# A planned order of steps replaced: LayerNorm, windowed attention and a gated layer on one core

## The chip, the core and the metric

The kernel runs on one core of a Trainium2 chip. The core has a matrix engine (TensorE, PE in the profile, with its weight loads as PEld), VectorE (DVE), ScalarE (ACT), GpSimd (POOL), and SyncE (SP), which here only issues DMAs. Each engine works through its own queue of instructions in order; an instruction that waits for another engine or for a DMA holds up all that stand behind it on its engine. The metric is the device time of one execution in microseconds.

## The reference

```python
h  = x + attention(layernorm(x)) @ wo       # x: 2048 x 512, 32 heads of 16
     # a query sees itself and the 255 keys before it
n  = layernorm(h)
h2 = h + (sigmoid(n @ w_gate) * (n @ w_up)) @ w_down     # 512 -> 1376 -> 512
```

All arrays are float32.

## The kernel before

**Numbers.** A float32 operand is held as two float16 halves: the cast (hi) and what the cast lost (lo). `mm3` (L356) does three matmuls for one product: hi·hi, hi·lo and lo·hi. So every operand needs a cast (L309 on ACT, L311 or, with a scale, L313 on DVE) and a subtraction (`subtract`, L316, on DVE or GpSimd; or, with a scale, a scalar_tensor_tensor on DVE: L752, L853, L966, L983).

**Attention.** The 2048 rows are cut into 8 blocks of 256 queries, and the heads into 8 groups. A block is normalized (`layernorm`, L489 to L504, then `split`), transposed, multiplied with wqkv (`do_qk`, `do_v`), and its rows are laid out anew through DRAM (`do_keys`, `do_queries`). For each half of the groups the scores are computed once with queries as rows (`do_s`, L652, tile sp), only to find each row's maximum (DVE, L639). `do_m` writes the maxima as two float16 halves (L659, L660), transposes them with a DMA (L664, tile mt) and puts them with a second DMA (L668) into spare rows of the queries' tile SQ. Then the scores are computed a second time with keys as rows (`do_st`: L703, L704, L705 and L714, tile stp), now with the maximum subtracted by the matmul itself. ACT takes exp (L681, tiles pa and pb), GpSimd zeroes what lies outside the window (`far`, L687, and `dia`, L692), and PE multiplies with the values (`do_pv`, L740, tile pvp, which has one buffer). Each of the 32 products of this kind is copied out as two halves rh ("raw": a cast, L309 or L313, then L752), which frees pvp for the next one. `do_o` transposes them back with a DMA (tile RT) and adds the halves (L770, tile OS). `do_wo` divides by the sum of the exps (L782, L784), splits the result (tile whl), transposes it with a DMA (tile oT, L533), multiplies with wo (L356, tile mmp) and adds the residual (L806).

**The second layer.** Its weights are split during the last attention block, once their largest value is known (`do_amax`, `scale`): w_gate through `do_T` (loads L952, cast, lo half L966 into tile Wg; four differences L976 on DVE or GpSimd, and their halves, L983, into Tg), w_up and w_down through `do_split` (tiles W0u and WD, L853). The first row tiles are normalized again (`do_ln2`) and multiplied with the first columns of both weights while attention still runs (`do_early`, tile sp from Wg and W0u). The other early products (`do_gu`) follow behind the last exp. From row tile 8 on, two tiles at a time go through `do_pair` and `do_group` (L1084), which does a 2 x 2 block product with 7 products instead of 8. `do_down` (L1244) multiplies with w_down, adds the residual (L1248) and stores.

**What sets the order.** Each of these pieces is a Python generator that yields once before each of its steps; with the yield it names the engines on which the step may run, what it needs, and what buffers it takes. The string `TABLE` (L64 to L224) lists all 4345 steps in order. `Order.run` reads it from left to right: a token is the name of a piece, a letter for the engine where there is a choice (a for ACT, v for DVE, g for GpSimd) and *n for n steps in a row.

```python
piece, (costs, needs, *rest) = self.live[name]
self.on = {"v": DVE_, "a": ACT_, "g": POOL_}[choice] if choice else next(iter(costs))
self.live[name][1] = piece.send(((0.0, self.on), *places))
```

No scheduler moves anything afterwards: the order of the table is the order on every engine. The costs that a piece yields, such as `4 * (n * 0.0031 + 0.15)` at L973 for the four subtractions L976 on GpSimd, were read by the planner that wrote the table. Here only the keys of `costs` are read.

Of the kernel before, what the change touches and what calls it, by code (L numbers as in the profile page):

```python
# [56 lines left out]
PE_, DVE_, ACT_, POOL_, DMA_ = ENGINES = "PE", "DVE", "ACT", "POOL", "DMA"  # L57
# [7 lines left out]
load_x0 load_x1 load_w0 load_w1 load_w3 load_w2 load_w4 load_w8 load_w9 load_x3 load_x2 load_w5 load_w10 load_w11 ln0 fill1 zeros0 ln0 ln1 load_w13 load_w7  # L65
load_w6 load_w15 load_x4 load_w14 load_x8 load_w12 load_x5 load_x6 ln0/a prep0/a ln0/a prep0/v*2 prep0/a prep0 ln1 ln0/v ln1/a prep0 warm1 ln0 ln1/a prep1/a
prep0 prep0/a ln0/v fill0*2 zeros1 ln1/g warm4 ln1 ln4 prep0 prep0/a prep0 prep0/a prep2/a prep0 ln1/a prep0/a prep0 ln4 ln4/v ln2 ln3 ln2 ln5 ln2/v prep2/a
warm3 qk0*2 qk1*2 qk0*3 qk1*2 qk0*3 ln3 prep1/a prep2/a*2 qk0/a prep2 ln3/v qk0 ln3/v ln2/a ln5 ln2/g ln3/g qk1*2 warm2 qk1*2 warm5 prep2 ln2 warm0 qk1/a qk1
prep1/a*2 ln2/v prep1 ln6 prep3/v prep2 warm7 ln3 prep1 warm6 queries2 queries0*2 queries3*3 queries1 queries2 load_x7 queries1*2 queries2 queries0 prep3/a*2
ln3/a qk4*5 qk5 qk4*3 qk5*6 ln4/a prep3/a prep2/a*2 prep2/g prep2/v ln7 prep3 prep2/v prep1 ln8 prep2/g fill2 prep2/a qk4/a prep2/a prep2/g fill2*4 ln4/g  # L70
prep2/v qk4 qk5 prep3*2 qk5/a prep2/a prep1/a qk5 v2*3 v0 prep2/v v2 v0 prep1 prep3/a prep1/a prep1 prep1/a prep1 v2/a prep1/a prep1 v0 qk3 warm8 qk3*2 v0 qk3
ln5/v v0/v qk3*3 qk2*2 qk3 qk2 queries5*2 amax0 queries7 amax2 queries7 amax1 queries7 queries4 queries6 queries4 queries6 queries4 queries6 qk2*5 qk3/a qk2/a
qk3 qk7*6 fill1 ln6 fill0*2 qk2 qk6 qk7*2 amax0/a qk7/v qk7 prep3/a prep3/g prep3/v keys0*2 amax3 queries5 keys0 qk6*6 v1 qk6 qk6/a v1*2 qk6 prep3/v amax2/v
ln9 prep3/v amax3/v prep3/v*2 v3 v1 v1/a amax1/a v3*2 ln4 v3 ln5/a ln4/a v3/a ln9 ln5/g ln8 fill1 ln7 ln6/a s0*3 s0.0 s0 s0.1 s0.2 s0*2 s0.3 s0.4 s0.5 s0*2 v4
s1 s0.6 s0.7 s1.0 amax4 keys1*2 keys0 amax6 s1*2 ln5 s1.1 s1.2 s2 s2.0 ln10 v4 s1 s1.3 s1*2 v4*2 s1.5 s1.4 open_work0 s1 s1.6 s1 s2 amax4/a ln6/a ln5/a ln10
ln6/g prep3/g v4/a ln7/a prep3/a s1.7 s2 s2.1 s2.2 qk8 s2 qk8 s2 s2.3 s2 qk8 s2.4 s2 s3 qk8 s2.5 qk8 s3 s2.6 qk8 s3.0 qk8 s3 s2 qk8 prep3/a qk8/a amax6/a ln11
s3.1 s3.2 s2.7 s3 qk9 s3*2 qk9 s3.3 s3.4 s3.5 s4 s4.0 s3 s3.6 qk8 qk9 s3 qk9*4 s4 qk9 s3.7 s4 qk10 s4 qk10 m0 s4.1 s4.2 s4.3 qk10 s4 s4.4 s4 qk10 s4 qk10*2 s4
qk10*2 amax7 qk9/a qk9 keys1 amax5 amax8 qk10/a amax5/a amax7/a m0*2 qk11 s4.5 s5 qk11 s4.6 s4.7 s5 qk11 s5.0 s5*2 qk11 qk10 qk11 s5.1 s5.2 qk11 s5 s6 qk11
s5.3 s5.4 s6.0 s5 qk11 s5.5 s6 s5 s6.1 s5.6 s5 s5.7 st0*2 ln6 qk11/a st0.0 st0.1 qk11 s6*2 st0 s6 st0 s6.2 ln7/a st0.2 st0.3 s6.3 s6.4 s6 s6.5 keys2*2 amax9
keys1 amax8/v amax11 st0*2 s7 s6*2 s7.0 s6.6 s6.7 ln6/a st0.5 ln7/g fill1 st0.4 v5 s7 st0.6 s7 st1 s7.1 s7.2 s7 ln7 st1 s7 st1.0 s7.3 s7 ln8/v s7.4 s7.5 st1  # L80
# [205 lines left out]
def tile_block(ctx, tc, x, wqkv, wo, wg, wu, wd, out):  # L286
# [1115 lines left out]
    n = 0  # L1402
# [54 lines left out]
```

## Time and profile before

| | |
|---|---|
| time, median of 3 runs | 781.17 us (779.52 to 781.47) |
| the profiled execution: its own time | 779.84 us |
| its span in the trace | 777.8 us |
| mean granted clock of PE | 0.993 |
| instructions | 18094 |
| busy: PE, DVE, ACT, POOL | 742.5, 600.7, 424.4, 346.8 us |

The span is the time between the first and the last instruction of the profiled execution; 2.0 us of its time lie outside. An engine's busy time is the time in which it worked at an instruction, waiting left out. A stretch of the span is given as a pair of times from its start. The granted clock is the share of full speed at which PE was allowed to run: 1.00 is full speed. In a row of the groups stand the line, the engine, the operation, what is written and read with its shape, the count, then the busy time and the mean in ns of one, and at last the idle time before them and what ended it. In a row of the waits stand the waiting engine, tile and line, behind the arrow what it waited for, then total, times and longest. In a row of the timeline stand start, duration, engine, line and, in brackets, the idle time just before.

### The profile page before, as it was taken

How to read it: one execution, taken by the hardware profiler on the slowest of the kernel's cores; microseconds unless marked ns; L12 is line 12 of the kernel's file. 1: busy time of each engine (PE TensorE's matmuls, PEld its weight loads, DVE VectorE, ACT ScalarE, POOL GpSimd, SP SyncE). 2: the span in 40 equal slices, each digit the busy share in tenths (PEclk: the TensorE clock that was granted, in tenths of full speed). 3: DMA queues.
4: the chain of work that ended last, by engine and by line, in shares of the span. 5: the costliest groups of instructions: out<-in, count | busy, mean ns of one | idle time of the engine just before them, and what ended most of it. 6: DMA issues, size and time to landing. Idle time of an engine off the chain costs nothing.

```text
span 777.8 us, 18094 instructions
## 1 busy us (share of the span) xinstructions
PE 742.5 (95%) x6714; PEld 468.1 (60%) x6714; DVE 600.7 (77%) x1772; ACT 424.4 (55%) x744; POOL 346.8 (45%) x437
## 2 busy tenths in 40 slices
PE   4899999999999999999997889999999999999998
PEld 4667767777787687786764444454544454545453
DVE  6969999989797887888889989993675757476552
ACT  6836889777787687887776725542221212223210
POOL 7642647454454553456466746670521302412310
PEclk9999999999999999999999899999999999999999
DMA  9973664646837639356735656634444534345243
GB/s 326 241 207 109 142 108 113 144 117 153 180 98 182 126 65 163 84 88 113 125 84 142 147 123 189 155 70 95 90 97 68 126 64 106 58 95 108 55 75 88
DMA packets 168568, 95.68 MB, mean 123 GB/s; under 512 B 140640, under 2 KB 146784, under 8 KB 168480
## 3 DMA queue, kind: packets, MB, share of 16 engines
q1 hardware_dynamic: 168480, 94.54, 54.4%
q8 instruction: 52, 0.85, 0.5%
q14 instruction: 36, 0.29, 0.2%
HBM read 35.26 MB, written 13.11 MB: 62 GB/s over the span
## 4 chain that ended last, share of the span: by engine, by line
PE 77%; DVE 15%; issue 3%; DMA 2%; ACT 2%; POOL 1%; DVEq 0%; POOLq 0%; ACTq 0%
PE mmp L356 30%; PE pvp L740 10%; PE sp L1084 9%; PE sp L652 8%; PE stp L1084 7%; PE stp L714 3%; PE pvp L1084 3%; PE stp L704 3%; PE stp L703 2%; PE stp L705 1%; PE sp L356 1%; DVE junk L639 1%; DVE st L489 1%; DVE Wg L966 1%; DVE X L976 1%
## 5 line engine op out<-in xcount | busy, mean ns | idle before, releaser
L639 DVE CUSTOM_DVE_ANT_0 junk<-sp,mask 128x320 bf16<-128x320 f32 (+4 forms) x512 | 215.2, 466 | 32.3 <-PE sp L652 28.7
L681 ACT ACTIVATE pa<-stp,kappa 128x512 f32<-128x512 f32 (+1 forms) x256 | 156.0, 646 | 41.4 <-PE stp L705 37.2
L652 PE MATMUL sp<-SK,SQ 96*128 96x256 f16 (+3 forms) x960 | 126.9, 232 | 2.9 <-DVE mq L639 2.0
L1084 PEld LDWEIGHTS <-SQ 128*128 128x128 f16 x756 | 73.9, 98 | 75.4
L356 PE MATMUL mmp<-xT,W 128*128 128x256 f16 x768 | 109.1, 272 | 0.5 <-ACT xT L309 0.5
L356 PE MATMUL mmp<-WD,hT 128*128 128x512 f16 (+1 forms) x408 | 97.7, 379 | 0.3 <-DMA hT<-X 0.3
L681 ACT ACTIVATE pb<-stp,kappa 128x512 f32<-128x512 f32 x128 | 83.5, 686 | 20.8 <-PE stp L714 19.4
L652 PEld LDWEIGHTS <-SQ 96*128 96x128 f16 x960 | 79.2, 97 | 25.8 <-issue 9.6
L687 POOL TENSOR_SCALAR_AFFINE_SELECT pa<-pa 128x1024 f32<-128x1024 f32 x56 | 62.0, 1106 | 61.8 <-ACT pa L681 60.3
L356 PEld LDWEIGHTS <-W 128*128 128x128 f16 x768 | 70.1, 97 | 10.3 <-issue 1.3
L356 PEld LDWEIGHTS <-hT 128*128 128x128 f16 (+1 forms) x408 | 39.8, 98 | 46.1 <-DMA hT<-X 0.6
L740 PE MATMUL pvp<-pa,VT 128*17 128x128 f32 (+1 forms) x1408 | 63.7, 312 | 2.9 <-DVE rh L752 2.9
L704 PE MATMUL stp<-SQ,SK 100*128 100x256 f16 x224 | 60.2, 272 | 0.0
L692 POOL TENSOR_SCALAR_AFFINE_SELECT pb<-pb 128x512 f32<-128x512 f32 x64 | 42.4, 663 | 35.1 <-ACT pb L681 34.7
L705 PE MATMUL stp<-SQ,SK 100*128 100x128 f16 x256 | 55.6, 219 | 0.5 <-ACT pb L681 0.2
L740 PEld LDWEIGHTS pvp<-pa,VT 128*17 128x17 f32 x1408 | 38.3, 99 | 26.5 <-issue 4.3
L703 PE MATMUL stp<-SQ,SK 100*128 100x128 f16 x224 | 49.5, 221 | 4.5 <-ACT pb L681 2.1
L356 PE MATMUL mmp<-WO,oT 128*128 128x512 f16 x192 | 51.6, 386 | 1.9 <-DMA oT<-whl 1.9
L692 POOL TENSOR_SCALAR_AFFINE_SELECT pa<-pa 128x512 f32<-128x512 f32 x64 | 41.8, 655 | 24.2 <-ACT pa L681 24.0
L356 PE MATMUL mmp<-W,xT 128*128 128x512 f16 x192 | 50.1, 378 | 1.7 <-DVE sq L578 1.6
L714 PE MATMUL stp<-SQ,SK 100*128 100x256 f16 x256 | 48.0, 274 | 0.3 <-ACT pa L681 0.2
L356 PEld LDWEIGHTS <-x 128*128 128x128 f16 x288 | 27.9, 98 | 32.2 <-issue 6.0
(329 smaller groups left out, 1368.6 us busy)
## 6 DMA issues: line engine op xcount, KB each, us to landing
SQ<-sq SPq DMA_DIRECT2D x96, 128.0 KB
SK<-mem SPq DMA_DIRECT2D x16, 384.0 KB
chunk<-in_wd_dram SPq DMA_DIRECT2D x20, 256.0 KB
mem<-sk SPq DMA_DIRECT2D x8, 512.0 KB
out_dram<-WO SPq DMA_DIRECT2D x16, 256.0 KB
X<-in_x_dram SPq DMA_DIRECT2D x7, 512.0 KB
chunk<-in_wu_dram SPq DMA_DIRECT2D x12, 256.0 KB
xs<-X SPq DMA_DIRECT2D x10, 256.0 KB
```

The lines of the kernel that those rows point to most:

```text
L356: PE.matmul(ps, a_of(a, k), b_of(b, k), start=(k == 0 and i == 0), stop=(k == n - 1 and i == 2))
L639: V.tensor_tensor_reduce(out=junk[:, c0:], in0=ps[:, c0:], in1=mask[:, c0:], scale=1.0, scalar=-3.0e38, op0=ALU.add, op1=ALU.max, accum_ou ...
L652: PE.matmul(ps[:, col:col + k1 - k0], q, SK[0:96, (2 * a + hf) % 5, 4 * (p % 2) + j, k0:k1], start=True, stop=True)
L681: S.activation(dst, a, AF.Exp, scale=kappa)
L687: G.affine_select(out=f, in_=f, pattern=[[0, 8], [-1, 128]], compare_op=ALU.is_gt, fill=0.0, base=0, channel_multiplier=1)
L692: G.affine_select(out=p, in_=p, pattern=[[0, 4], [1, 128]], compare_op=ALU.is_ge, fill=0.0, base=0, channel_multiplier=-1)
L703: PE.matmul(a[:, 0:128], ks(k0, g, j), qs(b, g, j, 0, 128), start=True, stop=True)
L704: PE.matmul(a[:, 128:384], ks(k0 + 1, g, j), qs(b, g, j, 0, 256), start=True, stop=True)
L705: PE.matmul(a[:, 384:512], ks(k0 + 3, g, j), qs(b, g, j, 128, 256), start=True, stop=True)
L714: PE.matmul(a[:, u, :], ks(k0 + 2, g, j + u), qs(b, g, j + u, 0, 256), start=True, stop=True)
L740: PE.matmul(ps[32 * j:32 * j + 17, u, q0:q1], VT[:, kt % 6, 8 * j + g, :], w[:, j, c:c + q1 - q0], start=first, stop=last, skip_group_chec ...
L1084: PE.matmul(out, x7[p][0][:, kk, MATS[a], ha, :], mv, start=first and i == 0, stop=i == 5, skip_group_check=True)
```

## The change

The whole table is replaced by another one (165 lines become 167, so that a line number after the table is 2 larger in the new kernel). Both have the same 4345 steps. About a third of them stand in the same sequence, and some choices of engine differ. One cost of the planner is changed with it, which the kernel as it runs doesn't read.

```diff
-load_x0 load_x1 load_w0 load_w1 load_w3 load_w2 load_w4 load_w8 load_w9 load_x3 load_x2 load_w5 load_w10 load_w11 ln0 fill1 zeros0 ln0 ln1 load_w13 load_w7
...
+load_x0 load_w0 load_x1 load_w1 load_w2 load_w3 zeros0 load_x3 ln0 load_x2 load_w4 load_w13 load_w8 load_w5 ln1 ln0 fill0 ln1 prep0/a ln0/a prep0/v ln1/v
...
-        e, = yield {POOL_: 4 * (n * 0.0031 + 0.15), DVE_: 4 * (n / 960 + 0.08)}, ends
+        e, = yield {POOL_: 4 * (n * 0.0021 + 0.15), DVE_: 4 * (n / 960 + 0.08)}, ends
```

Three places show what the new table does between the 28th and the last raw copy, while the last attention block runs and the weights Wg, Tg and W0u are split. The first is VectorE's queue around the last pieces of Wg (L966), shortly before the last raw copy but one. X is here the room of row tiles that are not in use, which holds normalized rows and their halves. Before:

```order
L966 SCALAR_TENSOR_TENSOR Wg<-X,sg,Wg 128x2x256 x2
L770 TENSOR_TENSOR OS<-RT 128x2x8x17
L313 TENSOR_SCALAR Wg<-X,sg 128x2x256
L966 SCALAR_TENSOR_TENSOR Wg<-X,sg,Wg 128x2x256 x2
L976 TENSOR_TENSOR X<-X 128x256 x4
L752 SCALAR_TENSOR_TENSOR rh<-pvp_94,rh 128x2x256
L504 TENSOR_SCALAR X<-X,mv,rs 128x512
L313 TENSOR_SCALAR W0u<-chunk_70,su 128x512
L983 SCALAR_TENSOR_TENSOR Tg<-X,sg,Tg 128x2x256
L311 CAST X<-X 128x512
L853 SCALAR_TENSOR_TENSOR W0u<-chunk_70,su,W0u 128x512
L316 TENSOR_TENSOR X<-X 128x512
```

After, with line numbers that are 2 larger:

```order
L968 SCALAR_TENSOR_TENSOR Wg<-X,sg,Wg 128x2x256 x3
L315 TENSOR_SCALAR Wg<-X,sg 128x2x256
L968 SCALAR_TENSOR_TENSOR Wg<-X,sg,Wg 128x2x256
L978 TENSOR_TENSOR X<-X 128x256 x4
L754 SCALAR_TENSOR_TENSOR rh<-pvp_94,rh 128x2x256
L808 SCALAR_TENSOR_TENSOR X<-mmp,co,X 128x512
L318 TENSOR_TENSOR X<-X 128x512
L855 SCALAR_TENSOR_TENSOR W0u<-chunk_72,su,W0u 128x512
L985 SCALAR_TENSOR_TENSOR Tg<-X,sg,Tg 128x2x256
L855 SCALAR_TENSOR_TENSOR W0u<-chunk_70,su,W0u 128x512
L313 COPY SQ_77<-sp 128x512
L754 SCALAR_TENSOR_TENSOR rh<-pvp_94,rh 128x2x256
```

Before, two casts for the halves of X and W0u and a normalization (L311, L313, L504) stand between the weights' pieces; now casts of the same kind are ACT's, and a subtraction (L318, which was L316) and a residual (L808) stand there. The raw copy (L752, now L754) stands behind the same four subtractions of `do_T` as before.

The second is GpSimd's queue at the end of the last attention block. Before:

```order
L497 TENSOR_SCALAR nb<-mv,rs 128x1
L692 AFFINE_SELECT pa<-pa 128x4x128
L692 AFFINE_SELECT pb<-pb 128x4x128
L316 TENSOR_TENSOR X<-X 128x512
L770 TENSOR_TENSOR OS<-RT 128x2x8x17
L687 AFFINE_SELECT pa<-pa 128x8x128
L692 AFFINE_SELECT pa<-pa 128x4x128
L692 AFFINE_SELECT pb<-pb 128x4x128
L976 TENSOR_TENSOR X<-X 128x256 x4
L770 TENSOR_TENSOR OS<-RT 128x2x8x17
L1310 MEMSET X 128x2x32
L770 TENSOR_TENSOR OS<-RT 128x2x8x17
```

After:

```order
L694 AFFINE_SELECT pb<-pb 128x4x128
L689 AFFINE_SELECT pa<-pa 128x8x128 x2
L694 AFFINE_SELECT pb<-pb 128x4x128
L689 AFFINE_SELECT pa<-pa 128x8x128
L694 AFFINE_SELECT pa<-pa 128x4x128
L694 AFFINE_SELECT pb<-pb 128x4x128
L497 TENSOR_TENSOR rs<-rs,nhalf 128x1
L499 TENSOR_SCALAR nb<-mv,rs 128x1
L694 AFFINE_SELECT pa<-pa 128x4x128
L689 AFFINE_SELECT pa<-pa 128x8x128
L694 AFFINE_SELECT pb<-pb 128x4x128
L978 TENSOR_TENSOR X<-X 128x256 x4
```

Before, a subtraction of X (L316) and the sums of `do_o` (L770) stand between the selects; now the selects follow each other, the normalization's two small steps (L497, L499) between them, and the four subtractions of `do_T` (L978, which was L976) are again at the end.

The third is TensorE's queue ahead of the 31st of the 32 products with the values (weight loads are left out). Before:

```order
L356 MATMUL mmp<-WO,oT 128x512
...
L714 MATMUL stp<-SQ_85,SK 128x256
...
L740 MATMUL pvp_94<-pa,VT 17x256 x4
L740 MATMUL pvp_94<-pa,VT 17x128 x8
L740 MATMUL pvp_94<-pb,VT 17x256 x4
```

After:

```order
L358 MATMUL sp<-Wg,x_7775 128x512
...
L716 MATMUL stp<-SQ_85,SK 128x256
...
L358 MATMUL mmp<-WO,oT 128x512
...
L742 MATMUL pvp_94<-pa,VT 17x256 x4
L742 MATMUL pvp_94<-pa,VT 17x128 x8
L742 MATMUL pvp_94<-pb,VT 17x256 x4
```

Before, four matmuls of scores stood between those with wo and the product; now an early product (three matmuls sp from Wg) and three of wo's stand there as well. From the 28th to the last raw copy 28 such early matmuls stood in the queue before, and 34 stand there now.

More of the change, by code (lines that the diff above doesn't have):

```diff
@@ L69 @@
[L69 to L80, printed above, removed]
@@ new lines @@
+prep3/a*2 prep3 prep1 ln7 queries0 queries3 prep2/a prep2/g fill2*2 prep2/a qk5 load_x7 load_x6 queries2 queries0 queries1 queries2*2 queries3 queries1*2
+queries0 prep1/v qk4/a qk5 prep2/a prep2/g qk5*4 qk5/a prep2/v prep2/a prep2/g fill0 qk4 qk5 prep3 prep1 queries7 queries4 queries5 v2*3 prep1/a prep1 prep1/a
+prep3 prep1 prep1/a prep1 v0 queries6 amax0 amax1 queries4 queries6 queries3 v0 v2 v0 v2/a v0 qk3*2 warm8 qk3*4 v0/v qk2 qk3*2 ln8 qk3/a qk3 ln4/v amax0/a
+ln5/a queries5 queries6 amax2 qk2*3 prep3/a amax1/a qk2*4 qk7 qk2/v qk7*2 qk2 ln9 qk7 prep3/a fill0 prep3/g prep3/a qk7 keys0 qk7 keys0 qk7*2 v1 queries7
@@ new lines @@
+s27.2 s27 wo3 amax18 ln10 o8 st20.3 amax20/a qk16/a st20.6 wo3 s26 s27 s27.3 s26.7 wo3 s28 s27 st20 s27.4 s28 pv9 wo2 st20.7 amax22 s27.5 wo3 s28.0 qk16
+amax23/a ln11/a amax24 st21 qk17*2 st21 qk17 s28 s27 st20.5 st20.8 s28.1 pv9/a st21.0 s27.6 s28.2 qk17 st21 st21.1 st21 s27 wo2 st21.2 s28*2 st21 amax18/v
+s27.7 st21.3 qk17 st21 wo2 pv10 s28.3 s29 m6 amax22/v s28.4 st21.6 s29.0 st21.7 ln11/g st21.8 st21.4 st20.4 s29 st22 qk17 s28 st22 qk17 s28 st22.0 s29.1 m6
+amax25 amax26 s28.5 s28 st22 st22.1 ln11 s29 wo2 st22 s28.6 st22.2 qk17 s29 s28.7 pv9 s29 st22.3 o9 m6 wo2 s29.2 qk17/a s29.3 st21.5 st22.4 o8/g o9/g st22.5
@@ new lines @@
+s50.5 qk30 s51 s50.6 st44.6 qk30 s51.0 st44 s51 s50 st44.7 st45 s51.1 s51 qk30 s50.7 st45.0 s51 st44.5 st44.4 o20/g st44.8 st45 qk31 st45.1 s51 st45 s51.3
+s51.2 st45.2 qk30 st45 s52 qk30 s51 s51.4 pv21 o21 st45.3 s52.0 st45 qk30 s51 st45.6 s51.5 st45 queries29 queries28 s51.6 s51 qk31 st45.7 s51.7 st46 st45.4
+st45.5 s52 qk30 queries28 queries30 st46.0 s52.1 st46 st45.8 wo9/g pv22 s52*3 st46 pv22 qk30/v wo9/a st46.1 st46.2 s52.4 s52.3 qk30 m12 s52.2 m12 st46 s53
+st46.3 s52 st46 pv22/v s53.0 s52.5 st46.6 qk31 s52 st46 st46.4 o21/g s52.6 qk31 m12 queries30*2 st46.7 st47 s53*2 st47.0 s53 st46.8 st46.5 st47 qk31 pv22
@@ new lines @@
+group0*2 group1.0/a T8 group1.2/a gu7/a pair1 group0.3/v pair1 pair1/v*2 group1.1 pair1/v group0.4 pair1 group0.5 pair1 group0.4 gu7/g down0 gu7 group1
+group1.4 group1.4/v group1.4/g group1.4 down1 pair1/g group0 group1 group2 group0.7 down3 group1 down3 group1.3/v group1.5 group0.6 down2 group1 group2*2
+group2.0/a group2 down3 pair1/v group2.1 group2 group2.2/a group2 group2.3/v group1.6 group2.5 group2 group2.4 pair1/g pair1 group2.4 down3 group1.7 group3
+pair2 group0.6 group2.7*2 group0.7 group1.7 group3.0/a group0.5 group3 down4 group4*2 group3 group2.6 group2.5 group2.6*2 group1.5 group1.5/a group2.7 group4
@@ new lines @@
+down4 group3.2/a group1.6 group4.0/a group4 group3 group3.1 pair2 group3 group4.2/a group1.6/a pair2 group2.5 group1.7/v group4.1 group1.7/g down4 group3
+group4 group3.3/g down3 group1.7 pair2*2 group1.6/g group3.5*2 group1.5/v group2.6 group2.6/a pair2 group3.4*2 group3 down5 group5 group4 down4 group3.7
+group1.6 down4*2 down5 group5 group2.5 group3.6 group1.5 pair2/g group5 down4*2 down5 group2.6/g group2.6 down5 down4 group2.5/a group2.5/v pair2/v down5*2
+group4.3/g group4.5 down5 down4 down5 group4 group2.5 down5 group5.2/v pair2/g pair2 down2 pair2 pair2/v pair2/a group3.6 group4.4 group5.0/a group5 down4
@@ new lines @@
+group9.7 group11.4 group10.7 group12*2 down9 group10.7 group10.7/a group11.2/a group9.5 group11.3/g group10.6 group11.5 group12 down8*2 group13 group11*2
+down10*3 group12.0/v group11.7 group13 group12 group10.5 group10.6/v*2 group10.5/v pair5 group10.6 group12.2/a group11.7 group11.6 group12.1 group11.6
+group11.5 group11.7 group11.5*2 down10 group13 group12.4 group11.6*2 group11.6/v pair5 group12.4 group13.2/a group13.0/a group10.7/g group12.3/g group10.7
+group13.1 pair5 down10 group12 down10 group12 group13 down11 group14 pair5 group12.5 group12 group13 down10 down11 down10 down11 group13 group12.6 pair5
@@ new lines @@
+group10.5/g group10.5 pair5 group11.6/v group14.0/v pair5/g pair5/a pair5/v group13.4 down9 group11.6 down8 group12.6 group12.5 group12.7 group14 down11
+down10 group14 pair5*2 pair5/g down10*2 down11 group14 down11*3 group13.6 group13.3/v group13.6 group11.5/v pair5/v group13.5 group14.1 pair5/g group13
+group14 group13.4/v group14.2/v group14 pair5 group13.5 group11.5/g group14.3/g group13.4/g group13.4 group13.5/v group13.7 down10 group15 group14.4*2 group16
+group15 down12*2 group15 group15.0/v group14.5 group14 group14.7 group15.1 down12 group15 group16 group13.6/a group13.6/v group14.6 group15.4*2 group16
@@ new lines @@
+group17 group17.3/v group16.6 group16.7 group17 down12*2 down13*3 group14.5 group16.7 group17.4 group16.7/a group17.5 down13*2 group17 down13 down12 down14
+group17 down13 group16.6 down14 down13*2 group16.6/v*2 group16.7/g group16.7 group16.5 down11 group16.6 group17.7 down14*2 group17.4 group17.7 group17.5
+group17.6 group17.7 group17.5 group17.6*3 group17.5 group17.5/a group17.5/g group17.6/v down13 group17.6/v group17.5 down12 down13 group17.6 down15*3 down14*2
+down15*3 down14*3 down15 down14 down15 down14 down15*2 down14 down15 down14 down15*2
```

274 lines of the change are left out of this document (128 added, 146 removed).

## The prediction

> **What bounds the kernel now.** I read the totals first, then a table of stretches, then the waits of the one stretch that stands out, then its instructions.
>
> ```profile
> span 777.8 us, 18094 instructions
> PE 742.5 (95%) x6714; PEld 468.1 (60%) x6714; DVE 600.7 (77%) x1772; ACT 424.4 (55%) x744; POOL 346.8 (45%) x437
> ```
>
> PE is busy for 95% of the span, so at most 35.3 us (777.8 − 742.5) can be won by a better order alone. Where they lie is shown by the busy time of each engine by stretch (the columns after the stretch: its length, PE, PEld, DVE, ACT, POOL busy, the granted clock, the DMA share, GB/s):
>
> ```profile
> 0.00:60.00 60.00, 45.82 (x391) 35.24 (x392) 44.95 (x123) 37.76 (x75) 38.21 (x58) 1.00 0.88 257
> 60.00:120.00 60.00, 56.41 (x630) 44.21 (x628) 58.05 (x275) 46.26 (x95) 27.11 (x39) 1.00 0.58 125
> 120.00:400.00 280.00, 279.55 (x3673) 209.80 (x3671) 236.58 (x907) 216.83 (x370) 146.37 (x188) 1.00 0.59 122
> 400.00:460.00 60.00, 48.06 (x477) 27.25 (x474) 56.75 (x104) 37.30 (x58) 37.11 (x43) 0.91 0.53 117
> 460.00:520.00 60.00, 58.96 (x296) 28.81 (x295) 56.48 (x88) 29.18 (x43) 38.03 (x41) 1.00 0.56 146
> 520.00:760.00 240.00, 239.72 (x1196) 116.69 (x1195) 144.09 (x274) 55.70 (x102) 59.06 (x69) 1.00 0.43 89
> 760.00:778.00 18.00, 13.98 (x65) 6.15 (x63) 3.76 (x8) 1.34 (x4) 0.86 (x1) 1.00 0.35 81
> ```
>
> From 120 to 400 (attention) and from 520 to 760 (the second layer) PE is idle for 0.45 and 0.28 us: no order of the same matmuls is faster there. The start leaves 14.2 us to loads and first casts, the tail 4.0. What is left is 400 to 460, the handover: the last attention block ends while the weights of the second layer are split. There PE is idle 11.9 us, DVE is busy 56.75 of 60, and the clock fell to 0.91. The handover proper runs from the end of the 28th of the 32 raw copies (L752), at 401.9, to the end of the last, at 457.3; the stretch behind it ends at 524.5 with the first down:
>
> ```profile
> 401.90:457.30 55.40, 43.46 (x446) 24.78 (x445) 52.15 (x94) 35.43 (x56) 36.96 (x42) 0.91 0.53 120
> 457.30:524.50 67.20, 65.88 (x332) 32.18 (x330) 62.88 (x99) 30.49 (x46) 41.04 (x47) 1.00 0.58 147
> ```
>
> DVE works 52.15 of those 55.40 us. What PE waits for there (total, times, longest):
>
> ```profile
> PE sp L356 <- DVE Wg L966: 3.4, 2, 1.8
> PE pvp L740 <- DVE rh L752: 2.9, 1, 2.9
> PE stp L703 <- ACT pb L681: 2.1, 1, 2.1
> ```
>
> The two largest, 6.3 us, wait for DVE. The timeline shows why DVE was late for the second:
>
> ```profile
> 447.44 3.35 DVE L976 TENSOR_TENSOR X<-X 128x256 f32<-128x256 f32 x4
> 448.75 3.67 POOL L976 TENSOR_TENSOR X<-X 128x256 f32<-128x256 f32 x4
> 450.71 0.68 DVE L752 SCALAR_TENSOR_TENSOR rh<-pvp,rh 128x512 f16<-128x512 f32 x1
> 451.53 1.91 PE L740 MATMUL pvp<-pa,VT 128*17 128x256 f32 x24 [2.90 <-DVE rh L752]
> ```
>
> Four DVE subtractions take 3.35 us with GpSimd beside them, 0.84 each, against 0.647 for the mean of the twelve here. The groups of the handover tell the same of other operations:
>
> ```profile
> L966 DVE SCALAR_TENSOR_TENSOR Wg<-X,sg,Wg 128x512 f16<-128x512 f32 x8 | 8.1, 1051 | 0.0
> L853 DVE SCALAR_TENSOR_TENSOR W0u<-chunk,su,W0u 128x512 f16<-128x512 f32 x4 | 3.0, 742 | 0.0
> L976 DVE TENSOR_TENSOR X<-X 128x256 f32<-128x256 f32 x12 | 7.8, 647 | 0.3
> L504 DVE TENSOR_SCALAR X<-X,mv,rs 128x512 f32<-128x512 f32 x4 | 3.9, 963 | 0.1
> L316 DVE TENSOR_TENSOR X<-X 128x512 f16<-128x512 f32 x2 | 2.2, 1088 | 0.0
> L316 DVE TENSOR_TENSOR whl<-OS,whl 128x512 f16<-128x512 f32 x1 | 1.4, 1428 | 0.0
> L316 POOL TENSOR_TENSOR X<-X 128x512 f16<-128x512 f32 x2 | 3.0, 1503 | 4.7 <-ACT X L309 4.7
> ```
>
> L966 and L853 are the same operation on the same shape, 1051 against 742 ns: DVE loses time to GpSimd, per instruction. Its shortest specimens, with little beside them:
>
> ```profile
> 451.31 0.53 DVE L504 TENSOR_SCALAR X<-X,mv,rs 128x512 f32<-128x512 f32 x1
> 454.29 0.68 DVE L316 TENSOR_TENSOR X<-X 128x512 f16<-128x512 f32 x1
> ```
>
> So DVE's loss here is at least L966 8 × (1.051 − 0.742) = 2.5, L504 4 × (0.963 − 0.53) = 1.7, L316 2 × 1.088 + 1.428 − 3 × 0.68 = 1.6, and L976, taking 0.53 as its bare time (my choice: it has half L504's elements but two inputs), 12 × 0.12 = 1.4: together 7.2 us.
>
> **The change part by part.** The planner's cost of L973 is read by nobody when the table runs, so it costs nothing. The table keeps every step, 4345 of them, and moves nearly all.
>
> *Engines in the handover.* Between the same two raw copies the new order has on DVE two fewer casts of X (L311), one fewer of whl, two fewer of W0u and one fewer of Wg (L313), and two fewer normalizations (L504), which go to ACT; and two more subtractions of X and one of whl (L316), which come from GpSimd, and two more row maxima (L639). More rows of the same view:
>
> ```profile
> L639 DVE CUSTOM_DVE_ANT_0 junk<-sp,mask 128x320 bf16<-128x320 f32 x5 | 2.3, 487 | 0.3 <-PE sp L652 0.3
> L313 DVE TENSOR_SCALAR W0u<-chunk,su 128x512 f16<-128x512 f32 x2 | 1.4, 710 | 0.0
> L311 DVE CAST X<-X 128x512 f16<-128x512 f32 x3 | 1.3, 419 | 0.0
> L692 POOL TENSOR_SCALAR_AFFINE_SELECT pb<-pb 128x512 f32<-128x512 f32 x8 | 6.6, 822 | 2.4 <-ACT pb L681 2.3
> L687 POOL TENSOR_SCALAR_AFFINE_SELECT pa<-pa 128x1024 f32<-128x1024 f32 x8 | 9.3, 1167 | 9.1 <-ACT pa L681 9.1
> L770 POOL TENSOR_TENSOR OS<-RT 128x272 f32<-128x272 f16 x3 | 2.9, 979 | 2.1 <-DMA RT<-rh 2.1
> ```
>
> Off DVE: 2 × 0.419 + 0.71 (whl's and Wg's cast taken at W0u's 0.710) × 4 + 2 × 0.963 = 5.6. Onto DVE: 2 × 1.088 + 1.428 + 2 × 0.487 = 4.6. Net −1.0. GpSimd loses 3 × 1.503 (whl's subtraction taken at X's), one L687 (1.167), one L692 (0.822) and two L770 (1.96): −8.5 of its 36.96 us, 23%. If DVE's 7.2 us of loss goes with the time GpSimd works beside it, another −1.7. Bounds: with the three new L316 each as slow as 1.428 and no smaller loss −0.3; with them at 0.68 (−1.6 more than the −1.0) and half the other losses of 5.6 gone, −5.4. I take −2.7, near the rows of this stretch. ACT takes six more operations of about 0.7 us, 4 us, with 20 us free in the stretch (55.40 − 35.43); that covers it unless they stand ahead of an exp.
>
> The Trainium skill, "SBUF — State Buffer", section "Who interferes with whom", states that VectorE and GpSimd share a pair of ports as an exclusive lock, held for a whole instruction by whoever issues first, and that a VectorE instruction with two inputs in SBUF contends with a GpSimd one that reads. The rows of L966, which has two such inputs, agree. By that rule a subtraction on DVE is the worse neighbour than the cast that it takes the place of, so it speaks against this half of the exchange.
>
> *More matmuls inside the handover.* The new order brings 34 instead of 28 early matmuls (sp from Wg) ahead of the last raw copy. From the timeline:
>
> ```profile
> 444.78 0.81 PE L356 MATMUL sp<-Wg,x 128*128 128x512 f16 x3
> ```
>
> 0.27 us each; six are 1.6 us that fill idle PE and are missing from the stretch behind, which PE sets (65.88 busy of 67.20). So −1.6, if that stretch stays PE's: DVE has 62.88 there, and the new order leaves DVE's work as it is (+0.1) while GpSimd's falls by about 10 us (both from the counts of the new order at the trace's mean durations), so DVE should not be later. Bounds 0 and −1.6; I take −1.6.
>
> *The clock.* The row of 400 to 460 has a granted clock of 0.91: 60 × 0.09 = 5.4 us of full-speed time are lost. If the idle time of 11.9 us falls by the 4.3 found above, a third, the loss may fall by as much, 1.9; I take half, −0.9, since single long waits, not their sum, may decide it. Bounds 0 and −5.4.
>
> *Everything else.* In attention and in the second layer PE has no idle time to win, and the new order, followed with the durations of this trace, leaves comparable distances between a group's products and its down. At the start the weights' last load of wk comes three places later; it is used some microseconds after landing either way. I take 0, with ±2 for what a new order can add or save there.
>
> Sum: −2.7 − 1.6 − 0.9 = −5.2. The profiled execution took 779.84 us (1.3 below the median of 781.17, and inside the runs' 779.52 to 781.47), so it would take 774.6; against the median **776.0**.
>
> **The rivals.** *No gain is passed on.* The three subtractions that move to DVE each wait out a select on GpSimd, 0.8 to 1.2 us by the rows of L692 and L687: that is about 3 us and takes back the 2.7. The clock stays, and of the early matmuls at most −1.6 remains: 779.5 at the median. For it: L316 on DVE took 1.088 and 1.428 here, 0.68 at its shortest. Against: those durations are in my sum already, and three subtractions fewer on GpSimd leave fewer to collide with. PE's chain from scores to exp to select would give the same, if it and not DVE sets the pace; for that speaks the third row of waits, 2.1 us for an exp.
>
> *Slower: the transfer of the row maxima.* Each half block's maxima go through a transposing DMA and a second DMA (L664, L668) before its first scores (L703) can start. The first two rows are from the chain of waits near 100 us, the third from the waits between 60 and 120, the last two from the handover's timeline:
>
> ```profile
> 101.25 4.65 DMA mt<-mh
> 105.91 2.10 DMA SQ<-mt
> PE stp L703 <- DMA SQ<-mt: 0.5, 1, 0.5
> 406.79 0.56 DVE L660 SCALAR_TENSOR_TENSOR mh<-mq,mh 128x32 f16<-128x32 f32 x1
> 413.66 1.13 SPq L668 DMA_DIRECT2D SQ<-mt  x2
> ```
>
> The chain takes 4.65 + 2.10, about 7.0 us with its issues; in the handover the second DMA issues 6.3 us after L660 ended at 407.35, and with 2.1 more that is 8.4. PE must have that much other work. Adding up the matmuls between L660 and the first L703 at the trace's mean durations, the new order leaves less at four of the sixteen: 3.97 (was 4.24), 6.98 (9.40), 6.86 (8.68) and 5.47 (7.74). At 7.0 the last waits 1.5 and the others next to nothing new; at 8.4 the last three wait 1.4, 1.5 and 2.9, and the first up to 4.4, 3.9 more than the 0.5 seen. That is +9.7 against −5.2: +4.5, 785.7. Slower by over 0.3% it is from a sum of 7.5 us on. Against: only one of sixteen waits at all now, and between L660 and L703 PE has waits of its own that use the time up.
>
> *The half clock goes.* If no wait in the handover is long enough for it, all 5.4 us return instead of 0.9, and the stretch follows: 776.0 − 4.5 = 771.5, and with DVE's bound (−5.4 for −2.7) 768.8. For it: the clock is 1.00 in every other row of the stretches. Against: DVE's waits are 6.3 of 11.9 us of idle time, so others remain. The Trainium skill, "TensorE: Matmul & The Clock Gate", states that the clock halves after an idle window of about 3.4 us; the longest single wait in the rows above is 2.90, so the gate here answers to less than that page says, or to several waits together.
>
> *The ports are not it.* If L966 is slow for where its operands lie, GpSimd's 8.5 us matter to nobody: −1.0 − 1.6 − 0 on 781.17 are 778.6. Against it stands L976, 0.84 against 0.647 in one stretch of the timeline with GpSimd beside it.
>
> **How the numbers follow.** A change of 0.3%, 2.3 us, is about what a measurement of this kernel can tell from none. The forecast, 773 to 778: 0.40. Half clock gone, 768 to 773: 0.17. Ports not it, 778.6: 0.10, half of it beyond the bound. No gain passed on, 779.5: 0.14. Slower by the maxima or by as much at the start, 781 to 787: 0.19. Faster 0.40 + 0.17 + 0.05 = 0.62; within 0.3% 0.05 + 0.14 = 0.19; slower 0.19. The range reaches from 768.0, below which little is left, to 784.5, above which I leave about 0.1.
>
> **What would show it.** Right: the stretch between the same two raw copies falls from 55.4 to about 51, with GpSimd near 28 us in it, L966 and L976 below 1051 and 647 ns, more sp matmuls ahead of the last L740, and a clock above 0.91 there. Wrong: L316 on DVE at over 1.4 us with PE waits on L752 or L966 as long as now; waits of L703 on the DMA of SQ of over 1 us; waits on exps that take the freed time; or a loss before 60 us or in the second layer that is larger than what the handover wins.

## The result and the profile after

The changed kernel took 770.56 us (median of 4 runs, 769.71 to 770.82) against 781.32 us (4 runs, 779.52 to 781.67): a ratio of 0.9865, 95% interval 0.9848 to 0.9882, or 10.5 us less, plus or minus 1.3. Forecast were 5.2 us less and a range from 768.0 to 784.5. The direction was right and the place was right. The time lies inside the range, but below the 773 to 778 that the forecast itself was given: one term of the sum was much too small, and another came out for its stated cause only in part.

The head of the page of the changed kernel:

```profile
span 768.0 us, 18055 instructions
PE 739.6 (96%) x6714; PEld 466.6 (61%) x6714; DVE 586.5 (76%) x1767; ACT 429.5 (56%) x756; POOL 339.3 (44%) x428
```

The span is 9.8 us shorter, with PE's busy time only 2.9 us less. The table of stretches, first the ones cut at the same times as before, then those between the same events as in the prediction (from the 28th to the last raw copy, and from there to the first down):

```profile
0.00:60.00 60.00, 46.27 (x389) 35.41 (x390) 47.48 (x120) 35.22 (x70) 36.64 (x55) 1.00 0.86 259
60.00:120.00 60.00, 57.47 (x642) 44.87 (x644) 58.06 (x282) 47.21 (x99) 29.27 (x43) 1.00 0.48 123
120.00:400.00 280.00, 278.72 (x3654) 208.84 (x3657) 235.42 (x902) 216.45 (x367) 147.74 (x189) 1.00 0.56 120
400.00:460.00 60.00, 53.65 (x529) 29.96 (x522) 53.31 (x110) 46.73 (x74) 31.52 (x39) 1.00 0.65 155
...
402.00:449.60 47.60, 41.25 (x460) 24.13 (x459) 44.58 (x92) 40.50 (x65) 29.65 (x36) 1.00 0.62 146
449.60:515.10 65.50, 64.76 (x328) 31.80 (x327) 58.80 (x99) 36.61 (x57) 29.40 (x33) 1.00 0.61 152
515.10:768.00 252.90, 249.13 (x1235) 120.45 (x1232) 140.99 (x275) 52.15 (x99) 66.42 (x73) 1.00 0.40 86
```

The handover starts at 402.0 (before 401.9), takes 47.6 us instead of 55.4, the stretch behind it 65.5 instead of 67.2, and all the rest 252.9 instead of 253.3. So 7.8 us come from the handover, 1.7 from the stretch behind it, and 0.3 from everything else. DVE works 44.58 us in the handover instead of 52.15: it lost 7.6 us of work, the stretch 7.8. The clock is 1.00.

What PE waits for from 400 to 460 (total, times, longest):

```profile
PE stp L716 <- ACT pa L683: 2.3, 5, 0.7
PE stp L705 <- ACT pa L683: 1.8, 4, 0.6
PE mmp L358 <- DMA oT<-whl: 0.9, 1, 0.9
PE sp L358 <- DVE Wg L968: 0.8, 1, 0.8
PE pvp L742 <- DVE rh L754: 0.5, 1, 0.5
PE stp L705 <- ACT pb L683: 0.2, 1, 0.2
```

The waits for DVE went from 6.3 to 1.3 us, no wait is longer than 0.9, and no matmul waits for SQ's DMA. DVE's groups in the handover (lines are 2 larger than before):

```profile
L968 DVE SCALAR_TENSOR_TENSOR Wg<-X,sg,Wg 128x512 f16<-128x512 f32 x8 | 5.9, 789 | 0.0
L985 DVE SCALAR_TENSOR_TENSOR Tg<-X,sg,Tg 128x512 f16<-128x512 f32 x5 | 5.6, 1153 | 0.0
L978 DVE TENSOR_TENSOR X<-X 128x256 f32<-128x256 f32 x12 | 5.1, 422 | 0.3
L855 DVE SCALAR_TENSOR_TENSOR W0u<-chunk,su,W0u 128x512 f16<-128x512 f32 x4 | 4.1, 1034 | 0.0
L318 DVE TENSOR_TENSOR X<-X 128x512 f16<-128x512 f32 x4 | 3.4, 862 | 0.7 <-ACT X L311 0.7
...
L318 DVE TENSOR_TENSOR whl<-OS,whl 128x512 f16<-128x512 f32 x2 | 1.4, 684 | 0.0
...
L506 DVE TENSOR_SCALAR X<-X,mv,rs 128x512 f32<-128x512 f32 x2 | 1.1, 538 | 0.0
```

L968 is down to 789 ns from 1051 and L978 to 422 from 647, while L985 and L855, about 740 at their shortest, are at 1153 and 1034: the delays moved and shrank, they did not vanish. The timeline shows how the long operations got fast. DVE and GpSimd around 424 us:

```profile
420.18 1.22 POOL L694 TENSOR_SCALAR_AFFINE_SELECT pa<-pa 128x512 f32<-128x512 f32 x1 [2.19 <-ACT pa L683]
...
428.18 0.93 POOL L694 TENSOR_SCALAR_AFFINE_SELECT pa<-pa 128x512 f32<-128x512 f32 x1 [6.78 <-ACT pa L683]
```

```profile
420.17 3.10 DVE L968 SCALAR_TENSOR_TENSOR Wg<-X,sg,Wg 128x512 f16<-128x512 f32 x4
423.20 1.78 DVE L978 TENSOR_TENSOR X<-X 128x256 f32<-128x256 f32 x4
424.90 0.68 DVE L318 TENSOR_TENSOR X<-X 128x512 f16<-128x512 f32 x1
425.50 1.79 DVE L978 TENSOR_TENSOR X<-X 128x256 f32<-128x256 f32 x4
```

GpSimd idles for 6.78 us, waiting for exps, and DVE does much of its two-input work in just that gap, among it eight subtractions at 0.45 us each. Before, such four beside a busy GpSimd took 3.35.

### The profile page after: what moved, and what is told of

Its sections match the earlier page's. It is cut to its first block, busy times and chain, and to the rows that moved or that the text cites. A ratio compares the mean times of both kernels' runs of the same rounds, so it can differ in the third digit from the quotient of the medians.

```text
span 768.0 us, 18055 instructions
## 1 busy us (share of the span) xinstructions
PE 739.6 (96%) x6714; PEld 466.6 (61%) x6714; DVE 586.5 (76%) x1767; ACT 429.5 (56%) x756; POOL 339.3 (44%) x428
## 4 chain that ended last, share of the span: by engine, by line
PE 79%; DVE 12%; issue 4%; POOL 3%; ACT 2%; DMA 1%; DVEq 0%; POOLq 0%; ACTq 0%
PE mmp L358 31%; PE sp L1086 10%; PE pvp L742 9%; PE sp L654 8%; PE stp L1086 7%; PE stp L716 3%; PE pvp L1086 3%; PE stp L706 3%; PE sp L358 2%; PE stp L705 2%; DVE junk L641 2%; PE stp L707 1%; PE stp L358 1%; DVE Tu L985 1%; ACT pa L683 1%
## 5 line engine op out<-in xcount | busy, mean ns | idle before, releaser
L654 PE MATMUL sp<-SK,SQ 96*128 96x256 f16 (+3 forms) x960 | 129.2, 232 | 2.3 <-DVE mq L641 1.6
L358 PEld LDWEIGHTS <-W 128*128 128x128 f16 x768 | 70.2, 97 | 9.8 <-issue 1.0
L707 PE MATMUL stp<-SQ,SK 100*128 100x128 f16 x256 | 55.3, 218 | 0.5 <-ACT pb L683 0.2
```

The costliest lines, as they stand in the source:

```text
L358: PE.matmul(ps, a_of(a, k), b_of(b, k), start=(k == 0 and i == 0), stop=(k == n - 1 and i == 2))
L654: PE.matmul(ps[:, col:col + k1 - k0], q, SK[0:96, (2 * a + hf) % 5, 4 * (p % 2) + j, k0:k1], start=True, stop=True)
L707: PE.matmul(a[:, 384:512], ks(k0 + 3, g, j), qs(b, g, j, 128, 256), start=True, stop=True)
```

## The experiments

My theory after the result: DVE's delay by GpSimd, not DVE's count of operations, is what the new table reduces, by where it puts the work. Rivals: the clock; the choices of engine alone, or the order alone; the early matmuls. Since both tables hold the same steps, a kernel can follow one table up to some step and the other from there on. All times stand in one table here; "handover" and "behind" are the two stretches of each one's profiled execution, with ends at tenths of a us; ratios are against runs of the kernel before on the same chip (medians of 780.44 to 781.82). "Excess" is what DVE's instructions of the handover took above their shortest durations, summed; the shortest duration is the shortest twentieth of each line and shape in the traces before and after. The expectations call it port loss.

| kernel | handover, us | excess in it, us | behind, us | time, us | ratio, 95% interval |
|---|---|---|---|---|---|
| before | 55.4 | 13.6 | 67.2 | 781.32 | 1 |
| after | 47.6 | 6.8 | 65.5 | 770.56 | 0.9865 (0.9848 to 0.9882) |
| mid_after | 47.5 | 5.7 | 69.5 | 774.13 | 0.9914 (0.9893 to 0.9935) |
| mid_engines | 55.2 | 11.8 | 68.4 | 781.12 | 0.9997 (0.9982 to 1.0011) |
| mid_order | 51.7 | 10.5 | 70.2 | 777.28 | 0.9949 (0.9935 to 0.9964) |
| late_after | 54.8 | 13.8 | 65.0 | 777.12 | 0.9953 (0.9933 to 0.9973) |
| late_engines | 55.3 | 13.5 | 73.1 | 800.98 | 1.0243 (1.0224 to 1.0261) |
| late_order | 54.5 | 13.4 | 67.6 | 787.75 | 1.0075 (1.0057 to 1.0093) |
| spin | 55.0 | 13.8 | 69.8 | 780.23 | 0.9994 (0.9980 to 1.0009) |
| after_again | 47.6 | 6.8 | 65.6 | 770.29 | 0.9864 (0.9839 to 0.9888) |
| pool_read | 51.6 | 10.6 | 65.7 | 774.44 | 0.9920 (0.9891 to 0.9949) |
| pool_set | 47.7 | 6.7 | 65.6 | 770.66 | 0.9866 (0.9840 to 0.9891) |
| t3_dve | 48.4 | 5.8 | 64.9 | 769.69 | 0.9855 (0.9839 to 0.9872) |
| t_all_dve | 48.4 | 5.9 | 66.4 | 771.74 | 0.9883 (0.9866 to 0.9899) |

**mid_after: the handover alone.** The tables are joined at the cast of the 28th raw copy and at that of the last.

```diff
-pv27/v wo8 st57.1 st57 s63.1 s63 wo8 st57.2 st57 s63.3 pv27 s63.2
-...
-T3/g last_exp0 pv31/a
+pv27/v st56.5 st56.4 s63.1 pv27 o27 st57.1 st56.8 o26/g wo8 st57 wo8 s63
+...
+T2 split0 pv31/a
```

> Before's table up to the 28th raw copy, the new table from there to the last raw copy, then before's again. If the whole gain is made in the handover: that stretch at 47 to 49 us instead of 55.4, the clock there at 1.00, and 772 to 774 us (ratio 0.988 to 0.991). If the gain needs the new order behind the handover as well, 775 or more. If what stands ahead of the handover prepared it (other DMAs, other buffers in use), the stretch stays above 52 us.

Measured 774.13, with the handover at 47.5 us. Its two stretches:

```profile
403.20:450.70 47.50, 40.99 (x455) 23.55 (x453) 43.30 (x91) 39.81 (x64) 29.82 (x36) 1.00 0.58 141
450.70:520.20 69.50, 66.20 (x325) 32.11 (x324) 66.68 (x99) 30.64 (x46) 41.58 (x48) 0.98 0.57 142
```

The whole saving of the handover is made by the handover's own order and choices. But behind it before's order takes 69.5 us here, 2.3 longer than in the trace before: DVE is busy 66.68 of them, and PE waits for ACT and DVE to split w_up:

```profile
PE stp L355 <- ACT W1u L308: 2.5, 1, 2.5
PE stp L355 <- DVE W1u L965: 0.8, 1, 0.8
```

The wait does not need the shorter handover. spin (below) has before's order throughout and a handover of 55.0 us, and behind it 69.8 us with the same wait:

```profile
PE stp L353 <- ACT W1u L306: 2.5, 1, 2.5
PE stp L353 <- DVE W1u L963: 0.4, 1, 0.4
```

With before's order the stretch behind takes 67.2 to 70.2 us in five kernels' profiled executions. Those of mid_after (775.36) and spin (783.32) are the slowest of their kernel's runs, that of before (779.84) is one of its faster, so such differences are partly between executions.

**mid_engines: the choices alone**, and **mid_order: the order alone**, in the handover. The eleven choices are eight casts or normalizations (DVE to ACT) and three subtractions (GpSimd to DVE); the expectation sorts them a little otherwise. mid_engines has before's order with the new choices; mid_order is mid_after with this edit undone (the eleven tokens alone, in their order):

```diff
-wo12/v wo12/g T1/v ln21/g ln22/v*2 ln22/g ln23/v split0/v ln23/v split1/v
+wo12/a wo12/v T1/a ln21/v ln22/a*2 ln22/v ln23/a split0/a ln23/a split1/a
```

> Before's order, and only the eleven choices of engine that differ in the handover taken from the new table: six casts or normalizations from DVE to ACT, two subtractions from GpSimd to DVE, three that stand elsewhere in the stretch. If the load on the shared port is what matters (my theory, engines): DVE at about 48 us busy in the stretch, the stretch 3 to 5 us shorter, 776 to 778 us. If it is the order of the operations on DVE and GpSimd that matters: within 1.5 us of 781. If the clock decides by a threshold: 1.00 or 0.91, nothing between, and the time follows it.

> The new order in the handover, with before's choices of engine for the same eleven steps. The engines' theory: most of the gain is lost, 777 or more, and the port loss of DVE (13.6 us before, 6.8 after) stays near 12. The order's theory: 772 to 776 with a port loss of 8 or less. The clock's theory (early matmuls fill the gaps): 1.00 and 772 to 775 whatever DVE does.

The choices alone gave nothing, where the theory of the engines had 776 to 778. The order alone gave 3.7 us of the handover's 7.8: its 777.28 is as the engines' theory had it, its excess of 10.5 lies between the two theories. Both together gave all of it. mid_engines shows why:

```profile
401.80:457.00 55.20, 43.70 (x449) 25.15 (x447) 49.13 (x88) 40.22 (x64) 33.21 (x39) 0.91 0.48 116
```

```profile
PE stp L701 <- ACT pa L679: 4.8, 5, 3.8
PE pvp L738 <- POOL pa L690: 3.8, 1, 3.8
PE pvp L738 <- DVE rh L750: 1.4, 1, 1.4
PE stp L701 <- ACT pb L679: 1.2, 2, 1.0
```

DVE was relieved of 3.0 us (49.13 against 52.15; the prediction had 2.7), and PE waits for two other things as long instead. The first, 3.8 us for an exp, is in ACT's timeline:

```profile
411.79 0.69 ACT L679 ACTIVATE pa<-stp,kappa 128x512 f32<-128x512 f32 x1 [1.89 <-PE stp L703]
415.47 0.63 ACT L307 ACTIVATE whl<-OS 128x512 f16<-128x512 f32 x1 [2.99 <-DMA oT<-whl]
416.01 2.03 ACT L679 ACTIVATE pa<-stp,kappa 128x512 f32<-128x512 f32 x3
```

The cast of whl, now ACT's, waits 2.99 us for the DMA that reads whl's one buffer, and three exps wait behind it in ACT's queue. The prediction had named this condition ("unless they stand ahead of an exp"), and the new order avoids it. No run moves this cast alone. The second wait of 3.8 us, ahead of the 31st product, ends with a select of GpSimd at 440.53 us; DVE's 30th raw copy ends at 440.49, 3.5 us later than before, so DVE was as late there. As to the clock: it is 0.91 here, and 0.99 in mid_order's handover, which is still 4.1 us longer than the changed kernel's. The rival that the clock alone decides falls with that.

**late_after, late_engines, late_order: the same split behind the last raw copy.** late_after follows before's table to the cast of the last raw copy, the new one after it. late_engines has before's order with the 90 new choices from there on, late_order the new order with before's. The first steps behind the joint in late_after:

```diff
-T3/a pv31 o30 ln23 o31 o30/g split1 T3*2 T2 early0*3 open_p20 split5
+o30 ln23 T3/a pv31 split1 o31 T3 T2 early0 early1 early0 early1 T3 open_p20 o30/v
 ...
```

> Before's table to the last raw copy, the new one behind it. If the 1.7 us that the stretch from the last raw copy to the first down became shorter are the early matmuls done ahead of it: no gain, 781 +- 1. If they come from the new order behind the handover, or if GpSimd's 11 us less work there counts: 779 to 780.

> Before's order everywhere; the 90 choices of engine that differ behind the last raw copy are the new table's (24 of them before the first down's end: casts from DVE to ACT, subtractions from GpSimd to DVE). If GpSimd's 11 us less work beside DVE is what shortened the stretch behind the handover: 65 to 66 us for it instead of 67 to 68, DVE's port loss there 9 to 10 us instead of 13 to 17, 777 to 779 us. If choices without order bring nothing, as in the handover: 780 to 782.

> The new order behind the last raw copy with before's choices of engine. If the choices carry the gain of 4 us that the new order and choices gave together: 780 to 782, port loss 13 us or more. If the order carries it: 777 to 778, and then GpSimd's load is not what counts there.

late_after is 4.7 us faster than before by the medians (777.12 against 781.82 on that chip; by the ratio 0.0047 x 781.82 = 3.7), with the handover as before. Its two stretches:

```profile
401.20:456.00 54.80, 42.65 (x455) 24.56 (x454) 52.20 (x93) 35.87 (x56) 36.74 (x41) 0.97 0.57 118
456.00:521.00 65.00, 64.19 (x326) 31.52 (x324) 58.91 (x99) 36.16 (x56) 29.00 (x33) 1.00 0.63 156
```

That is more than the 779 to 780 expected. Behind the handover DVE works 58.91 us instead of 62.88 and GpSimd 29.00 instead of 41.04. This stretch is short with the new table (64.9 to 66.4 us in seven profiled executions) whatever the handover was, and longer with the old one (67.2 to 70.2). The ratios of mid_after and late_after multiply to 0.9867, the whole effect. Half of the recipe is worse than none: late_engines is 19.6 us and late_order 6.3 us slower than before, which neither expectation foresaw. DVE's excess behind the handover came about as expected, 7.8 us in late_engines and 13.9 in late_order (13.5 before, 9.2 after), but it doesn't set the time there. In late_engines PE waits for DMAs, of oT and of the pairs' rows (SQ from OS), from 457 to 770; late_order loses its time behind the first down, 262.4 us against 253.3:

```profile
PE stp L1082 <- DMA SQ<-OS: 6.3, 2, 5.0
PE mmp L354 <- DMA oT<-whl: 5.0, 1, 5.0
```

**spin: the clock.** Before's table with idle matmuls on PE ahead of three long waits of the handover.

```diff
+def spin():
+    while True:
+        e, n = yield {PE_: 0.45}, [], ["mm"]
+        pt = psum_tile("mm", [P, 512])
+        for _ in range(8):
+            PE.matmul(pt[:, :P], identh, identh, start=True, stop=True)
+        plan.free("mm", n, e)
...
```

> Before's table with 15 sets of eight idle 128-wide matmuls (120 in all, read by nobody) put on PE ahead of the waits of 2.1, 1.8 and 2.9 us in the handover, so that PE is not idle there. If the half clock set the time, as my rival had it: granted clock 0.98 or more from 400 to 460, and 3 to 5 us saved, 776 to 778. If DVE set it: the clock rises as well, but the stretch stays at 54 to 57 us and the time within 2 us of 781.

The time did not change. The part of the handover from the 29th to the 30th raw copy had the half clock before; in spin it has the full one. First before, then spin:

```profile
418.80:437.00 18.20, 13.19 (x121) 7.41 (x119) 17.68 (x30) 12.58 (x21) 9.41 (x10) 0.81 0.75 153
```

```profile
403.20:458.20 55.00, 49.18 (x570) 31.82 (x569) 52.40 (x94) 35.75 (x56) 36.91 (x42) 0.94 0.54 119
420.10:439.80 19.70, 16.60 (x208) 11.70 (x206) 19.18 (x30) 16.31 (x27) 13.14 (x13) 1.00 0.67 149
```

At full clock it took 19.7 us, at 0.81 it took 18.2, and DVE is busy 19.18 and 17.68 of these: the clock does not set this part. (The idle matmuls may delay PE's own by some of the 1.5 us.) Over the whole handover spin's clock is only 0.94, since it fell at other waits, so the test holds for this part; late_after's handover, the same order as before at 0.97 and 54.8 us, points the same way, and so does mid_order's. Behind the handover PE is busy nearly all the time, and no run tests the clock there: in mid_after's 69.5 us at 0.98 about 1.4 us of full-speed time are lost (69.5 × 0.02).

**pool_read and pool_set: the port.** The changed kernel with work for GpSimd, read by nobody, in the gap of 6.78 us: eight subtractions, or 18 memsets. after_again is the changed kernel beside them.

```diff
+def spare():
+    for _ in range(8):
+        e, = yield {POOL_: 1.1}, ["x2p"]
+        G.tensor_tensor(out=dum[0], in0=dum[0], in1=dum[0], op=ALU.subtract)   # pool_set: 18 of G.memset(dum[0], 0.0)
...
```

> The changed kernel once more, for comparison with the two below on the same chip: 770 to 771, ratio 0.985 to 0.988.

> The changed kernel with eight subtractions of 128x256 float32 on GpSimd, read by nobody, in the gap of 6.8 us at 421 to 428 in which GpSimd idles and DVE splits weights (L966, L976). They keep GpSimd busy for about 6 us and delay no select by more than 1 us. If DVE loses time to GpSimd through the port: L966 there back from 0.78 to over 0.95 us and L976 from 0.45 to over 0.6, DVE 2 to 4 us later, the time 1.5 to 4 us longer than the changed kernel's. If the slow DVE operations of before had another cause: both at their short durations and within 1 us of the changed kernel.

> The same place with 18 memsets of 128x256 float32 instead: GpSimd is as busy, but writes and reads nothing. If what DVE waits for is GpSimd's reading: DVE's two-input operations there keep their short durations, and the time is within 1 us of the changed kernel's. If any work of GpSimd, or the place that it takes in GpSimd's queue, costs: as slow as with the subtractions.

With the subtractions on GpSimd the time is 4.2 us longer than after_again's, with the memsets the same. The same instructions of DVE in pool_read:

```profile
420.46 3.82 DVE L966 SCALAR_TENSOR_TENSOR Wg<-X,sg,Wg 128x512 f16<-128x512 f32 x4
424.19 3.09 DVE L976 TENSOR_TENSOR X<-X 128x256 f32<-128x256 f32 x4
428.22 2.21 DVE L976 TENSOR_TENSOR X<-X 128x256 f32<-128x256 f32 x4
430.39 1.20 POOL L692 TENSOR_SCALAR_AFFINE_SELECT pa<-pa 128x512 f32<-128x512 f32 x1 [1.62 <-ACT pa L681]
```

The subtractions took 7.11 us, not the 6 expected, but the next select (last row) still waited 1.62 us for its exp, so their place in the queue did not delay it. And in pool_set, with GpSimd's row among them:

```profile
421.30 3.10 DVE L966 SCALAR_TENSOR_TENSOR Wg<-X,sg,Wg 128x512 f16<-128x512 f32 x4
422.48 6.57 POOL L1370 MEMSET dum<- 128x256 f32 x18
424.32 1.79 DVE L976 TENSOR_TENSOR X<-X 128x256 f32<-128x256 f32 x4
426.63 1.79 DVE L976 TENSOR_TENSOR X<-X 128x256 f32<-128x256 f32 x4
```

3.10 against 3.82 and 1.79 against 3.09: GpSimd busy with memsets, which read nothing, does not delay DVE, and GpSimd busy with subtractions, which read two operands, does. The delay goes into the time in full: the excess is 3.7 us larger, the handover 4.0 us longer. The Trainium skill, "SBUF — State Buffer", section "Who interferes with whom", states that a VectorE instruction with two inputs in SBUF contends with a GpSimd one that reads SBUF and not with one that only writes; both runs agree.

**t3_dve and t_all_dve: less of GpSimd still.** The changed kernel with its last four L976 of the handover, or all 24 that GpSimd has, on DVE.

```diff
-T3/g
+T3/v
```

> The changed kernel, with the last four subtractions L976 of the handover (4.57 us on GpSimd at 444 us) on DVE. By the subtractions read by nobody, one on GpSimd costs DVE about 0.36 us (2.9 us for eight), and one on DVE takes 0.45: no gain, 770 to 771.5. If GpSimd's work were the bound there: up to 2 us faster.

> All 24 subtractions L976 that the changed kernel has on GpSimd put on DVE. By the same prices DVE's own work grows by about 10 us and its port loss falls by about 8 in the 113 us: 770 to 773. If the loss to the port goes with all of GpSimd's work and weighs more than the work itself: 767 to 769.

769.69 and 771.74: the first is the changed kernel's time by its ratio, the second 1.4 us above after_again. In t_all_dve DVE's work at its shortest durations grows by 9.5 us over both stretches, and its excess falls by 5.6 (expected were 10 and 8): of these 24 subtractions, one on GpSimd costs DVE 0.23 us and one on DVE 0.40. So moving more of them off GpSimd gains nothing.

## Why the prediction was right or wrong

**The place and the mechanism: right.** The handover was bound by DVE in the main, and DVE was held up by GpSimd. pool_read and pool_set show it: GpSimd's reading alone puts 4 us back. The rival "the ports are not it" fell with them. And the sum closes: DVE's excess fell by 6.8 us and its own work by 0.6, against 7.6 us less of DVE's busy time and 7.8 us less of the stretch. mid_engines shows the limit: relieved of 3 us of DVE's work, the handover was as long as before, as other waits took their place.

**DVE's own operations, −1.0: about right.** At the shortest durations the work that DVE has in the handover sums to 43.2 us before and 42.6 after, −0.6; the −1.0 was summed at delayed means. ACT took eight operations more and not six, the prediction's own list has eight, and 5.1 us instead of 4; it had room.

**DVE's loss to the port, −1.7: the step that failed in size.** It said that the loss "goes with the time GpSimd works beside it". GpSimd's time fell about as forecast, from 36.96 to 29.65 (−7.3, forecast −8.5). But the loss, the excess of the table, fell from 13.6 us to 6.8, by half and not by 23%. Two errors are in it. The 7.2 us I started from were too low: L976's bare time, which I chose as 0.53, is 0.45 (1.79 / 4), and I left out the losses of other operations, the casts L313 (1.7 us in seven) and L770 (0.938 against 0.43 at its shortest) above all. And the loss depends on what stands beside what: the new table puts eight of the twelve L976 and most of four of the eight L966 into one gap of GpSimd (−2.7 and −2.1 us for all of them, by the groups' means), and leaves the delays to L983 and L853 (+1.7 and +1.2). mid_engines, with about half of GpSimd's reduction (33.21 us) and the old order, lost 11.8 us, near the 12.2 of an even share (13.6 × 33.21 / 36.96); the rest came with the new order. An even share of overlap is the wrong price for a table that keeps the two apart.

One reading of that step was wrong as well: the L504 of 0.53 us, taken as having "little beside" it, stands beside GpSimd's subtractions (448.75 to 452.42), so these did not slow it; why others of its kind were slower stays open.

**Six more early matmuls, −1.6 behind the handover: the number came, the cause only in part.** The stretch behind got 1.7 us shorter: PE is busy 1.1 us less in it (64.76 against 65.88) and idle 0.6 us less. But matmuls done earlier do not shorten it by themselves. mid_after, with the new table's 34 ahead of the last raw copy, has 69.5 us; late_order, where PE is busy 64.76 us as in the changed kernel, has 67.6, because PE waits for the splits of the weights and for a DMA. late_after, with before's 28 ahead of that copy in the queue, has 65.0. The step's own condition, "if that stretch stays PE's", is met only with the new order and the new choices behind the last raw copy: without them PE waits for w_up to be split (2.5 and 0.8 us in mid_after). How much of the 1.7 us is the six matmuls and how much the missing waits, no run separates.

**The clock, −0.9: not shown to be worth anything.** The half clock went altogether, as the rival with 771.5 had it, and the time fell into that rival's 768 to 773; but spin, mid_order and late_after say that in the handover it was a mark of PE's waiting and not what set the time. That the number is near the rival's is chance: the larger fall of DVE's loss made it up.

**The maxima's DMA, up to 785.7:** no matmul waits for SQ in the changed kernel's trace, though the new order has less work there. In the handover the first scores start at 416.15, 6.0 us after the end of L662 (410.17), less than the 7.0 and 8.4 that I had taken for the chain. It was close: the weight load just ahead of them waited 0.33 us for that DMA, and in pool_read's trace the scores there waited 0.7. **No gain passed on:** the subtractions that moved to DVE took 0.862 and 0.684, not 1.088 and 1.428; most of them, too, stand where GpSimd idles. The other half of that rival, PE's chain of exps, is what happened in mid_engines, where the same choices without the order met it.

**Everything else, 0 ± 2:** 401.9 to 402.0 ahead of the handover and 253.3 to 252.9 behind the first down.

## What to carry over

When an engine's operations take longer in one stretch than elsewhere on the same shape, sum that excess over the stretch before anything is costed: here 13.6 us of DVE's time, more than any operation that could be moved. What is won there depends on which instructions lie beside each other, so a set of moves between engines that is worth nothing by itself (0.9997), with one moved cast waiting ahead of the exps, was worth half of the handover's gain with another order. A stretch in which two engines are each busy above 90% has two bounds: before a gain of one is added, look at what the other will wait for.

## What the runs showed of the hardware

GpSimd's subtractions of 128x256 float32 beside DVE cost DVE 0.72 us on four L966 and 1.30 us on four L976; memsets of nearly the same total time (6.57 against 7.11 us) cost nothing (3.10 and 1.79 us, as without them). The eight subtractions took 0.89 us each there. The half clock came and went with PE's gaps, and a part of the handover that DVE set was no shorter without it: 18.2 us at a granted clock of 0.81, 19.7 at 1.00.
